# Attention's sums inverted as columns, expert weights split earlier, on one Trainium2 core

## The chip, the cores and the metric

One core of one Trainium2 chip runs the whole program. The metric is the device time of one execution in microseconds, taken as the median of the runs; in this kernel about 0.2% can be told from no change.

## The reference

```python
scores = q @ k.T / sqrt(64) + min(-(cum_i - cum_j), 0), causal    # cum: running sum of max(s, 0)
attn = exp(scores - max); attn = attn / (sum(attn) + 1e-9)
x = (attn @ v)                      # 4 batches, 8 heads, 576 positions, 64 per head
x = x.transpose(0, 2, 1, 3).reshape(2304, 512)
h = max(x @ w_in, 0); x = (h * h) @ w_out                         # 512 -> 2048 -> 512
h = max(x @ w1, x @ w2, x @ w3); out = h @ w_out2                 # 512 -> 768 -> 512
```

All inputs are float32, the weights come as 64-bit words (float64).

## The kernel before

**Attention** goes through 16 pairs of heads, each pair through nine units of 128 score rows (64 of each head for the ninth, unit 8). For a unit TensorE makes the scores (`u_s`, L508 to L518), VectorE adds the mask and takes the largest (`u_max`, L531), ScalarE takes the exponential in place and adds it up into a column of a small tile `sums` (`u_exp`, L545), TensorE transposes the exponentials into one of two PSUM banks (`u_t`, L590), and ScalarE copies them out as `et` (`u_et`, L617 to L622). Units 0 to 3 are window 0 of the pair, units 4 to 8 window 1. When a window is complete TensorE multiplies `et` with the values (`w_pv`, L642), and VectorE copies the product to `xT` (`w_out_`, L653).

The sums stand as columns, a row for a query. They are needed as rows. `u_t` transposes them (L597) into the last 64 columns of the bank that holds unit 5's, or unit 8's, exponentials; `w_cp` adds 1e-9 out of that bank (L556) and takes the reciprocal (L558), both on a tile of 4 or 5 rows and 128 columns; `w_keep` stores it in DRAM (L565, L567), `w_rows` fetches it back spread over 64 rows (L574), and `w_px` multiplies on GpSimd (L658).

The order is a table, `ORDER`: step n of the loop does, from left to right, each operation for unit n + d. `LOADS` says when the next pair's inputs are loaded, on the SP queue.

**The experts** work on `xT` in chunks of 512 or 384 tokens. Every float32 factor is split into a high part and a low rest in the type fp32r, and three products stand for one (`three`, L661). For tokens this is `split_x` (a cast on ScalarE, L665, a subtraction on VectorE, L666). The first stage goes through nine visits: chunks 0 to 3 with the first half of the 16 blocks of `w_in` and `w_out`, chunk 4 with all 16 (visit 4), chunks 3 to 0 with the second half. A block is an "h" step (12 products, L672) and, two steps later, an "x" step (12 products, L798). Between them: relu and square (L777, L778), split (L780, L781). At a visit's end the four sums are copied out (L808, L810). The second stage (L838, L879) has 24 weights. `first_split` and `first_products` do the first `PRE` = 2 "h" steps of chunk 0 at the end of attention.

**Weights.** A weight block becomes a split tile by a job (`w_job`) of nine stages: two loads, four steps on VectorE (L340 to L351) that turn the 64-bit words to a float, an addition (L355), a cast on ScalarE (L360), a subtraction (L363). The additions run on GpSimd during attention, on VectorE afterwards. An early job makes a second-stage weight in a spare tile and stores it to DRAM (L366); `w_bring` fetches it later on GpSimd's queue (L379). A planner, `Slots`, decides at each call of `pump`, when the program is written, which job goes a stage on and whether one begins: weights needed within `SOON` steps at once, others at most one per `pace`. Attention calls it in the steps of a pair that `PUMP_U` lists, and with `ADV_ATT` = 1 each call does one stage; the experts call it after every step.

## Time and profile before

| | |
|---|---|
| median of 3 runs | 896.93 us (896.42 to 897.15) |
| profiled execution | 896.98 us |
| its span | 895.2 us |
| TensorE, VectorE, ScalarE, GpSimd busy | 855.9, 514.3, 332.2, 66.9 us |
| granted TensorE clock, mean | 0.997 |

Times within the profile count from the span's start. Attention ends near 187 us, the first expert stage near 592, the rest is the second. A row of a timeline gives start, duration, engine, line, operation and, in brackets, how long the engine idled before and what released it. PE is TensorE, PEld its weight loads, DVE VectorE, ACT ScalarE, POOL GpSimd, SPq the SP queue.

### The profile page before, as it was taken

The numbers are of one execution on the slowest core, as the hardware profiler recorded it, in microseconds if no ns is written. First come the engines' busy times: TensorE is split into PE (matmuls) and PEld (weight loads), VectorE is DVE, ScalarE is ACT, GpSimd is POOL, SyncE is SP. The second block draws the span as 40 slices with busy tenths as digits, with TensorE's granted clock in tenths as the row PEclk, the third lists the DMA queues.
The fourth block names the chain that finished last, engine by engine and source line by source line (L and its number), as shares of the span: only waits on it lengthen the run. The fifth ranks groups of instructions, "written<-read, shape, count | busy, mean of one in ns | idle before, by whom it ended". The sixth has DMA issues, their size and how long they took to land.

```text
span 895.2 us, 14075 instructions
## 1 busy us (share of the span) xinstructions
PE 855.9 (96%) x5446; PEld 730.0 (82%) x5446; DVE 514.3 (57%) x1079; ACT 332.2 (37%) x729; POOL 66.9 (7%) x79
## 2 busy tenths in 40 slices
PE   5999888899899999998999999999999999999998
PEld 3555555577688899997998888899999999999997
DVE  6788797868886333788888777633223131312211
ACT  5788887843333223323333333311112120212111
POOL 2133333310000000000000000110000000000000
PEclk9999999999999999999999999999999999999999
DMA  4454545212321020432425355950000000000001
GB/s 144 152 151 126 177 125 166 86 57 94 125 88 47 1 83 1 142 95 94 130 69 196 116 190 184 318 151 1 13 24 1 36 1 36 1 25 12 12 24 36
DMA packets 45267, 79.00 MB, mean 88 GB/s; under 512 B 7568, under 2 KB 17360, under 8 KB 45200
## 3 DMA queue, kind: packets, MB, share of 16 engines
q1 hardware_dynamic: 42884, 69.70, 24.3%
q0 software_dynamic: 2304, 8.39, 3.1%
q8 instruction: 43, 0.70, 0.3%
q14 instruction: 24, 0.20, 0.1%
q10 hardware_dynamic: 12, 0.01, 0.0%
HBM read 60.84 MB, written 17.22 MB: 87 GB/s over the span
## 4 chain that ended last, share of the span: by engine, by line
PE 75%; DVE 14%; ACT 6%; issue 4%; DMA 1%; DVEq 0%; ACTq 0%
PE banks L838 17%; PE banks L798 16%; PE first L838 8%; PE banks L879 8%; PE first L672 8%; PE banks L672 8%; PE pairs L642 4%; PE pairs L590 3%; DVE e L531 2%; PE pair L508 2%; DVE st L351 2%; PE pairs L508 2%; DVE r L778 2%; ACT hh L780 2%; ACT et L619 2%
## 5 line engine op out<-in xcount | busy, mean ns | idle before, releaser
L798 PE MATMUL banks<-hh,sl 128*128 128x512 f32 (+1 forms) x840 | 187.1, 371 | 4.4 <-DVE pt L808 1.8
L798 PEld LDWEIGHTS banks<-hh,sl 128*128 128x128 f32 x840 | 153.9, 189 | 27.7 <-DVE pt L808 2.2
L838 PE MATMUL banks<-xs,sl 128*128 128x384 f32 x720 | 128.7, 334 | 0.0
L838 PEld LDWEIGHTS banks<-xs,sl 128*128 128x128 f32 x720 | 125.1, 188 | 0.0
L780 ACT CAST hh<-r 128x512 fp32r<-128x512 f32 (+1 forms) x80 | 46.2, 578 | 152.8 <-DVE r L778 152.8
L672 PE MATMUL banks<-xs,sl 128*128 128x512 f32 (+1 forms) x420 | 92.0, 367 | 0.0
L672 PE MATMUL first<-xs,sl 128*128 128x512 f32 (+1 forms) x396 | 87.2, 368 | 4.4 <-DVE xs L666 3.2
L545 ACT ACTIVATE e<-e,nm 128x128 f32<-128x128 f32 (+2 forms) x144 | 83.5, 582 | 11.9 <-DVE nm L531 11.5
L672 PEld LDWEIGHTS banks<-xs,sl 128*128 128x128 f32 x420 | 76.7, 188 | 9.9
L672 PEld LDWEIGHTS first<-xs,sl 128*128 128x128 f32 x396 | 72.3, 188 | 13.9 <-DVE xs L666 3.5
L781 DVE TENSOR_TENSOR hh<-r,hh 128x512 fp32r<-128x512 f32 (+1 forms) x80 | 51.1, 639 | 51.5 <-ACT hh L780 50.2
L854 DVE TENSOR_TENSOR r<-banks,r 128x384 f32<-128x384 f32 x54 | 30.1, 557 | 78.5 <-PE banks L838 78.0
L879 PE MATMUL banks<-sl,hh 128*128 128x512 f32 (+1 forms) x342 | 74.9, 378 | 0.0
L879 PEld LDWEIGHTS banks<-sl,hh 128*128 128x128 f32 x342 | 61.8, 188 | 11.8
L858 ACT CAST hh<-r 128x384 fp32r<-128x384 f32 x36 | 18.5, 513 | 138.4 <-DVE r L854 138.4
L590 PEld LDWEIGHTS pairs<-identF,e 64*128 64x128 f32 x800 | 33.4, 139 | 30.6 <-ACT et L619 23.2
L590 PE MATMUL pairs<-identF,e 64*128 64x64 f32 x800 | 41.4, 230 | 16.8 <-ACT et L619 16.5
L642 PEld LDWEIGHTS pairs<-et,xv 128*64 128x64 f32 (+1 forms) x448 | 27.8, 135 | 31.2 <-ACT e L545 8.3
L642 PE MATMUL pairs<-et,xv 128*64 128x320 f32 (+4 forms) x448 | 52.7, 367 | 0.0
L838 PE MATMUL first<-xs,sl 128*128 128x384 f32 x288 | 52.0, 335 | 0.0
L838 PEld LDWEIGHTS first<-xs,sl 128*128 128x128 f32 x288 | 50.3, 188 | 0.5
L854 DVE TENSOR_TENSOR r<-first,r 128x384 f32<-128x384 f32 x18 | 10.0, 558 | 67.3 <-PE first L838 67.3
(104 smaller groups left out, 1116.1 us busy)
## 6 DMA issues: line engine op xcount, KB each, us to landing
st<-in_w_out_dram SPq DMA_DIRECT2D x44, 256.0 KB
st<-in_w_dram SPq DMA_DIRECT2D x36, 256.0 KB
st<-in_w_in_dram SPq DMA_DIRECT2D x32, 256.0 KB
keep_w<-spare SPq DMA_DIRECT2D x10, 512.0 KB
xk<-in_kT_dram SPq DMA_DIRECT2D x16, 288.0 KB
xq<-in_qT_dram SPq DMA_DIRECT2D x16, 288.0 KB
out_dram<-ob SPq DMA_DIRECT2D x17, 256.0 KB
xv<-in_v_main_dram SPq DMA_DIRECT2D x16, 256.0 KB
```

Of the source, the lines that this page charges most:

```text
L508: nc.tensor.matmul(b[:, j, 0:w], lhsT=d["xq"][rows(j), w - P:w], rhs=d["xk"][rows(j), 0:w], start=True, stop=False)
L545: nc.scalar.activation(out=e_u[u][:, 0:w], in_=e_u[u][:, 0:w], func=ACTF.Exp, scale=-1.0, bias=st.pop(n), accum_out=sums[p, win][:, col:co ...
L590: nc.tensor.transpose(t[:, h, at * D:(at + 1) * D], e_u[v][rows(h), k * P:(k + 1) * P], identF[rows(h), rows(h)])
L642: nc.tensor.matmul(pv[rows(j), f:(W0, W1)[w]], lhsT=xv[0:kr, j, k, :], rhs=rhs, start=(k == 0), stop=(k == last))
L672: nc.tensor.matmul(hps[:, 0:n], lhsT=w[:, wp, kk * P:(kk + 1) * P], rhs=x[kk][xp][:, 0:n], start=(kk == 0 and c == 0), stop=(kk == KD - 1 ...
L780: nc.scalar.copy(out=hh[:, 0, 0:n], in_=r[:, 0:n])
L781: nc.vector.tensor_tensor(out=hh[:, 1, 0:n], in0=r[:, 0:n], in1=f32(hh[:, 0, 0:n]), op=ALU.subtract)
L798: nc.tensor.matmul(xacc[d][:, 0:n], lhsT=w[:, wp, d * P:(d + 1) * P], rhs=hh[:, xp, 0:n], start=(m == 0 and c == 0), stop=(end and c == 2))
L838: nc.tensor.matmul(pj[j][:, 0:n], lhsT=w[:, wp, kk * P:(kk + 1) * P], rhs=xs[kk][xp][:, 0:n], start=(kk == 0 and c == 0), stop=(kk == KD - ...
L854: nc.vector.tensor_tensor(out=r[:, 0:n], in0=p[:, 0:n], in1=r[:, 0:n], op=ALU.max)
L858: nc.scalar.copy(out=hh[:, 0, 0:n], in_=r[:, 0:n])
L879: nc.tensor.matmul(po[:, 0:hi - lo], lhsT=hs[ci, f][:, hp_, t * P:(t + 1) * P], rhs=w[:, wp, lo:hi], start=(c == 0), stop=(c == 3 * NF2 - 1))
```

## The change

Six things are done.

- The sums become reciprocals while they are columns (`w_rc`, on tiles of 128 x 4 or 5). One transpose per window behind the value products puts them into the second half of the product's bank, and `w_out_` copies them out behind the values.
- `w_keep` moves from unit offset -6 to -7, behind that copy.
- The planner is called in all nine steps of a pair (`PUMP_U`).
- Weights needed more than `FAR` = 24 steps ahead keep a pace of 3.
- Early jobs may run in every visit but 0, 1 and 4, where they could from the 81st step on (in visit 4).
- The first expert split is spread over attention's last 30 units, high part and low part in steps of their own; the first products begin one step earlier and go five per step, where they went three.

```diff
-PRE_X = 8
-PRE_AT = 0
-PRE_N = 3
-PUMP_U = (0, 2, 3, 4, 5, 7)
+PRE_X = (30, 21, 12, 5)
+PRE_AT = 1
+PRE_N = 5
+PUMP_U = range(9)
...
-EARLY_FROM = 80
+EARLY_NOT_IN = (0, 1, 4)
+FAR = 24
+PACE_FAR = 3
...
-ORDER = [("max", 1), ("cp", -3), ("out0", -6), ("out1", -7), ("exp", -1), ("et", -3), ("t", -2), ("s", 2), ("pv", -5), ("rows", -13),
-         ("pump", 0), ("keep", -6), ("px", -19)]
+ORDER = [("max", 1), ("out0", -6), ("out1", -7), ("rc", -3), ("exp", -1), ("et", -3), ("t", -2), ("s", 2), ("pv", -5), ("rows", -13),
+         ("pump", 0), ("keep", -7), ("px", -19)]
...
-                if n - self.pos > (SOON_KEPT if kept else SOON) and (kept or self.clock - self.last < self.pace):
+                pace = self.pace if n - self.pos <= FAR else max(self.pace, PACE_FAR)
+                if n - self.pos > (SOON_KEPT if kept else SOON) and (kept or self.clock - self.last < pace):
...
-        if not self.start() and self.idle_from is not None and self.pos >= self.idle_from and \
+        if not self.start() and self.pos in self.idle and \
...
-    def w_cp(p, w):
-        nu = U0 + w
-        sm = small.tile([NU - U0, P], F32, tag="rec", name="rec", bufs=2)
-        nc.vector.tensor_scalar(out=sm[0:nu, :].rearrange("u (h c) -> u h c", c=D), in0=tr_t.pop((p, w)), scalar1=1.0e-9,
-                                scalar2=None, op0=ALU.add)
-        nc.vector.reciprocal(out=sm[0:nu, :], in_=sm[0:nu, :])
-        rec_t[p, w] = sm
+    def w_rc(p, w):
+        sm = sums[p, w][:, 0:U0 + w]
+        nc.vector.tensor_scalar(out=sm, in0=sm, scalar1=1.0e-9, scalar2=None, op0=ALU.add)
+        nc.vector.reciprocal(out=sm, in_=sm)
...
-        if n in ends:
-            _, w = ends[n]
-            o = tr_t[p, w] = t[0:U0 + w, :, 7 * D:8 * D]
-            sm = sums.pop((p, w))
-            for h in range(2):
-                nc.tensor.transpose(o[:, h, :], sm[rows(h), 0:U0 + w], identF[rows(h), rows(h)])
...
+        sm = sums.pop((p, w))
+        nc.tensor.transpose(t[0:U0 + w, 1, 0:P], sm[:, 0:U0 + w], identF)
...
         nc.vector.tensor_copy(x, t[:, 0, 0:n])
+
+        sm = rec_t[p, w] = small.tile([NU - U0, P], F32, tag="rec", name="rec", bufs=2)
+        nc.vector.tensor_copy(sm[0:U0 + w, :], t[0:U0 + w, 1, 0:P])
         ring_t.give(t)
...
-            if n == N:
+            if n == N - PRE_AT:
                 phQ.close()
                 banks.extend(psum(ctx, "first", 2, [P, 512]))
-            if PRE and n >= N - PRE_X and (n - N + PRE_X) % 2 == 0 and (n - N + PRE_X) // 2 < KD:
-                first_split((n - N + PRE_X) // 2)
+            for kk in range(KD):
+                for later in range(2):
+                    if n == N - PRE_X[kk] + later:
+                        first_split(kk, later)
```

### Where instructions move

First place: ScalarE in the middle of attention, from the exponential of unit 6 to that of the next pair's unit 0. `et` are the copies of transposed exponentials, `e_152` to `e_154` the units 6 to 8. Before:

```order
L545 ACTIVATE e_152,sm_1221<-e_152,nm 128x512 [waits DVE_49]
L545 ACTIVATE e_153,sm_1221<-e_153,nm 128x512 [waits DVE_49]
L619 COPY et_1292<-pairs_91 128x2x6x64 [waits DVE_49,PE_49]
L545 ACTIVATE e_154,sm_1221<-e_154,nm 128x576
L545 ACTIVATE e_146,sm_1327<-e_146,nm 128x128 [waits Activation_49]
```

The change:

```order
L547 ACTIVATE e_152,sm_902<-e_152,nm 128x512 [waits DVE_49]
L364 CAST sl_69<-wa 128x512 [waits Pool_49]
L547 ACTIVATE e_153,sm_902<-e_153,nm 128x512 [waits DVE_49]
L609 COPY et_972<-pairs_91 128x2x6x64 [waits PE_49,Activation_49]
L547 ACTIVATE e_154,sm_902<-e_154,nm 128x576 [waits DVE_49]
L547 ACTIVATE e_146,sm_1012<-e_146,nm 128x128 [waits DVE_49,Activation_49]
```

The copy L619, L609 in the change, waits for TensorE and VectorE before, and for TensorE (and ScalarE itself) in the change.

Second place: the end of attention. First TensorE, from the transposes of the last unit (`e8`) to the first "h" step of the experts (`banks`); `first` are the banks of the first products. Before:

```order
L590 MATMUL pairs0_90<-identF_139,e8_154 128x64 x9
L597 MATMUL pairs0_90<-identF_139,sm1_2698 5x64 x2
L672 MATMUL first0_2787<-sl18_85,sl0_67 128x512 x3
...
L642 MATMUL pairs1_91<-et1_2757,xv_2552 64x320 x5
...
L672 MATMUL first1_2788<-sl18_85,sl1_68 128x512 x3
L672 MATMUL first1_2788<-sl17_84,sl1_68 128x512 x3
...
L672 MATMUL banks0_2865<-xs_2893,sl2_69 128x512 [waits DVE_49,Activation_49]
```

The change:

```order
L588 MATMUL pairs0_90<-identF_139,e8_154 128x64 x9
...
L673 MATMUL first1_2823<-sl18_85,sl1_68 128x512 x3
L673 MATMUL first1_2823<-sl17_84,sl1_68 128x512 x3
...
L632 MATMUL pairs1_91<-et1_2810,xv_2604 64x320 x5
...
L635 MATMUL pairs1_91<-identF_139,sm1_2756 5x128 [waits DVE_49]
L673 MATMUL banks0_2922<-xs_2950,sl2_69 128x512 [waits PE_49,Activation_49]
```

All 24 first products stand ahead of the last value products, where 12 stood behind them. On VectorE the same place reads, before:

```order
L556 TENSOR_SCALAR rec<-pairs_90 5x128 [waits DMAHW7_49,DMAHW6_49,PE_49]
L558 RECIPROCAL rec<-rec 5x128 [waits DVE_49]
L653 COPY xT<-pairs_91 128x320 [waits PE_49,Activation_49]
L666 TENSOR_TENSOR xs<-xT,xs 128x512 [waits DMAHW5_49,Activation_49]
L666 TENSOR_TENSOR xs<-xT,xs 128x512 [waits DMAHW5_49,DMAHW6_49,DMAHW2_49,Activation_49]
```

The change:

```order
L557 RECIPROCAL sm_2756<-sm_2756 128x5 [waits DVE_49]
L646 COPY xT<-pairs_91 128x320 [waits PE_49,Activation_49]
L649 COPY rec<-pairs_91 5x128 [waits DMAHW1_49,DMAHW0_49]
L663 TENSOR_TENSOR xs<-xT,xs 128x512 [waits DMAHW5_49,DMAHW4_49,Activation_49]
L663 TENSOR_TENSOR xs<-xT,xs 128x512 [waits DMAHW4_49,DMAHW7_49,DMAHW0_49,Activation_49]
```

The tile `rec` that goes to DRAM is complete before the last value copy in the one, behind it in the other. The second split of `xs` takes memory over from `rec` and waits, in both, for that store (the semaphores DMAHW).

Third place: VectorE at the end of visit 4 (the two splits in one row belong to its last block). Before:

```order
L348 TENSOR_SCALAR wa<-st 128x512
L351 SCALAR_TENSOR_TENSOR st<-st,wa 128x512
L355 TENSOR_TENSOR wa<-st 128x512
L340 TENSOR_SCALAR wa<-st 128x512
L344 SCALAR_TENSOR_TENSOR st<-st,wa 128x512
L666 TENSOR_TENSOR xs<-xT,xs 128x384 x2
L778 SCALAR_TENSOR_TENSOR r<-banks_2866,r 128x384
L781 TENSOR_TENSOR hh<-r,hh 128x384
L363 TENSOR_TENSOR sl_77<-wa,sl_77 128x512
L348 TENSOR_SCALAR wa<-st 128x512
```

The change:

```order
L663 TENSOR_TENSOR xs<-xT,xs 128x384
L367 TENSOR_TENSOR sl_74<-wa,sl_74 128x512
L782 SCALAR_TENSOR_TENSOR r<-first_2823,r 128x384
L785 TENSOR_TENSOR hh<-r,hh 128x384
L782 SCALAR_TENSOR_TENSOR r<-banks_2922,r 128x384
L785 TENSOR_TENSOR hh<-r,hh 128x384
L663 TENSOR_TENSOR xs<-xT,xs 128x384 x2
L782 SCALAR_TENSOR_TENSOR r<-banks_2923,r 128x384
L785 TENSOR_TENSOR hh<-r,hh 128x384
```

The weight work around the splits is gone there; it stands in visits 2 and 3, one job per two blocks, where there was none.

Over the program 56 jobs are made in both. On GpSimd, in attention, there are 15 of the additions L355 where there were 10, and 15 of the subtractions L363 where there were 9; 24 of the jobs are early ones where 16 were, and as many tiles are stored and fetched back.

## Rows read from the trace of the kernel before

**Rows 1.** The page: span of the profiled execution.

```profile
span 895.2 us, 14075 instructions
```

**Rows 2.** Windows of one pair each: length, then PE, PEld, DVE, ACT, POOL busy (14 windows).

```profile
161.43:173.38 11.95, 10.04 (x121) 5.83 (x118) 10.83 (x29) 8.91 (x22) 4.19 (x5) 1.00 0.38 107
...
sum 151.51, PE 135.87 PEld 80.92 DVE 123.89 ACT 123.20 POOL 49.97; mean PE 9.71 PEld 5.78 DVE 8.85 ACT 8.80 POOL 3.57
```

**Rows 3.** Groups by line, shapes apart, 22.59 to 186.82: busy us, mean ns, idle before.

```profile
L590 PE MATMUL pairs<-identF,e 64*128 64x64 f32 x746 | 38.5, 230 | 16.0 <-ACT et L619 15.7 <-ACT e L545 0.4
...
L558 DVE RECIPROCAL rec<-rec 4x128 f32<-4x128 f32 x15 | 14.1, 941 | 0.5
...
L619 ACT COPY et<-pairs 128x768 f32<-128x768 f32 x15 | 12.0, 799 | 12.9 <-DVE rec L556 11.3 <-PE pairs L642 1.6
...
L531 DVE DVE_READ_ACCUMULATOR2_ANT nm<- 128x1 f32 x130 | 9.9, 76 | 0.0
...
L351 DVE SCALAR_TENSOR_TENSOR st<-st,wa 128x512 f32<-128x512 uint32 x10 | 8.2, 816 | 0.0
...
L556 DVE TENSOR_SCALAR rec<-pairs 4x128 f32<-4x128 f32 x15 | 4.1, 274 | 0.2 <-issue 0.2
```

**Rows 4.** Timeline of ScalarE in the pair from 75.56.

```profile
81.08 0.80 ACT L619 COPY et<-pairs 128x768 f32<-128x768 f32 x1 [0.77 <-DVE rec L556]
```

**Rows 5.** The chain that ended last, in order of time: start, us, what.

```profile
249.59 2.72 PE first L672 x12
...
345.42 2.08 PE banks L672 x12
```

**Rows 6.** Timeline of TensorE at the end of visit 0.

```profile
217.56 2.88 PE L672 MATMUL banks<-xs,sl 128*128 128x512 f32 x12
221.08 3.38 PE L798 MATMUL banks<-hh,sl 128*128 128x512 f32 x12 [0.64 <-ACT sl L360]
...
241.81 2.34 PE L798 MATMUL banks<-hh,sl 128*128 128x512 f32 x9 [1.76 <-DVE pt L808]
243.98 2.88 PE L672 MATMUL banks<-xs,sl 128*128 128x512 f32 x12
```

**Rows 7.** Timeline of TensorE between visits 4 and 5; one window with its clock.

```profile
413.98 2.24 PE L798 MATMUL banks<-hh,sl 128*128 128x384 f32 x12
...
422.06 1.48 PE L672 MATMUL first<-xs,sl 128*128 128x384 f32 x5 [3.20 <-DVE xs L666]
...
436.64 0.68 PE L672 MATMUL banks<-xs,slb 128*128 128x384 f32 x3
...
424.00:426.00 2.00, 2.00 (x8) 0.50 0.00 0
```

**Rows 8.** Timeline of the engines at the end of attention.

```profile
182.62 0.94 DVE L558 RECIPROCAL rec<-rec 5x128 f32<-5x128 f32 x1
...
186.02 1.66 ACT L665 CAST xs<-xT 128x512 fp32r<-128x512 f32 x3 [2.18 <-DMA r<-rec]
...
186.82 2.35 PE L672 MATMUL first<-sl,sl 128*128 128x512 f32 x9
187.01 0.49 DVE L653 COPY xT<-pairs 128x320 f32<-128x320 f32 x1 [3.44 <-PE pairs L642]
187.41 3.72 DVE L666 TENSOR_TENSOR xs<-xT,xs 128x512 fp32r<-128x512 f32 x4
...
193.17 2.12 PE L798 MATMUL banks<-hh,sl 128*128 128x512 f32 x8 [0.23 <-DVE hh L781]
```

**Rows 9.** Groups by line over the whole run.

```profile
L351 DVE SCALAR_TENSOR_TENSOR st<-st,wa 128x512 f32<-128x512 uint32 x56 | 40.1, 716 | 1.6
...
L363 POOL TENSOR_TENSOR sl<-wa,sl 128x512 fp32r<-128x512 f32 x9 | 12.7, 1413 | 26.9 <-ACT sl L360 26.9
...
L355 POOL TENSOR_TENSOR wa<-st 128x512 f32<-128x512 f32 x10 | 10.4, 1039 | 19.4 <-DVE st L351 19.4
```

**Rows 10.** Window of visit 8: engines busy, clock, share of the transfer engines, GB/s.

```profile
560.00:570.00 10.00, 10.00 (x45) 8.27 (x45) 6.82 (x12) 2.90 (x6) 2.11 (x4) 1.00 1.05 353
```

More of the change, by code (lines that the diff above doesn't have):

```diff
@@ L107, in __init__ @@
         self.most = ADV_ATT
-        self.idle_from = None
+        self.idle = ()
     def add(self, tiles):
@@ L487 @@
     units = [(p, u) for p in range(NP) for u in range(NU)]
-    wins, ends = {}, {}
+    wins = {}
     for n, (p, u) in enumerate(units):
@@ L491 @@
             wins[n] = (p, int(u >= U0))
-        if u in (U0 + 1, NU - 1):
-            ends[n] = (p, int(u == NU - 1))
     st = {}
@@ L661, with high, low_of, split_x @@
     three = ((0, 0), (0, 1), (1, 0))
-    def split_x(t0, n, kk, high, low):
-        src = xT[:, kk, t0:t0 + n]
-        nc.scalar.copy(out=high[:, 0:n], in_=src)
-        nc.vector.tensor_tensor(out=low[:, 0:n], in0=src, in1=f32(high[:, 0:n]), op=ALU.subtract)
-        return high, low
+    def high(t0, n, kk, hi, lo):
+        nc.scalar.copy(out=hi[:, 0:n], in_=xT[:, kk, t0:t0 + n])
+    def low_of(t0, n, kk, hi, lo):
+        nc.vector.tensor_tensor(out=lo[:, 0:n], in0=xT[:, kk, t0:t0 + n], in1=f32(hi[:, 0:n]), op=ALU.subtract)
+    def split_x(t0, n, kk, hi, lo):
+        high(t0, n, kk, hi, lo)
+        low_of(t0, n, kk, hi, lo)
+        return hi, lo
     def h_products(hps, x, n, w):
@@ L677, with first_split @@
     first_x = {}
-    def first_split(kk):
-        if kk < HELD_BACK:
-            high, low = (slots_a[-1 - kk][:, i, :] for i in range(2))
-        else:
-            high, low = (hp.tile([P, S], F32R, tag=n, name=n)[:, 0:512] for n in ("xk", "xq"))
-        first_x[kk] = split_x(*chunks1[0], kk, high, low)
+    def first_split(kk, low):
+        if not low:
+            if kk < HELD_BACK:
+                first_x[kk] = tuple(slots_a[-1 - kk][:, i, :] for i in range(2))
+            else:
+                first_x[kk] = tuple(hp.tile([P, S], F32R, tag=n, name=n)[:, 0:512] for n in ("xk", "xq"))
+        (high if not low else low_of)(*chunks1[0], kk, *first_x[kk])
     def first_products():
@@ L695, in attention @@
         fns = dict(s=u_s, t=u_t, max=u_max, et=u_et, exp=u_exp)
-        efn = dict(cp=w_cp)
-        wfn = dict(pv=w_pv, out0=w_out_, out1=w_out_, keep=w_keep, rows=w_rows, px=w_px)
+        wfn = dict(rc=w_rc, pv=w_pv, pv0=w_pv, pv1=w_pv, out0=w_out_, out1=w_out_, keep=w_keep, rows=w_rows, px=w_px)
         span = max(abs(d) for _, d in ORDER)
@@ L715, in attention @@
                         slots.pump(1)
-                elif op in efn:
-                    if n + d in ends:
-                        efn[op](*ends[n + d])
                 elif op in wfn:
-                    if n + d in wins and op not in ("out1", "out0")[wins[n + d][1]]:
+                    if n + d in wins and op[-1] != "10"[wins[n + d][1]]:
                         wfn[op](*wins[n + d])
@@ L740, in experts @@
         adder[0] = nc.vector
-        slots.idle_from = EARLY_FROM
+        slots.idle = set(range(len(steps)))
+        for i, step in enumerate(main1):
+            if step[1] in EARLY_NOT_IN:
+                slots.idle.discard(i)
         slots.add(slots_a[-HELD_BACK:] + [sl_p.tile([P, 2, 512], F32R, name=f"slb{i}") for i in range(SLOTS_B)])
```

1 line of the change is left out of this document (removed).

## The prediction

> **What bounds the kernel now.** I read the page first, then the windows, the groups by line, and the timelines of the places where TensorE waits. The profiled execution took 896.98 us for a span of 895.2 us [rows 1], so 1.78 us lie outside the span; the median of the runs shown, 896.93, is the same within 0.05 us. Everything below is counted in the span and taken from 896.98. TensorE sets the end: a change is worth what it takes out of, or adds to, TensorE's own waits, and nothing else.
>
> Attention: between 33.28 and 184.79 us lie 14 pairs of heads of 151.51 / 14 = 10.82 us each; TensorE is busy for 9.71 of it, VectorE for 8.85, ScalarE for 8.80 [rows 2]. So 1.1 us per pair is lost, and the groups say to what: in the 15 pairs from 22.59 on, the transposes of exponentials (L590) wait 16.0 us, of that 15.7 for one copy on ScalarE, L619 [rows 3]. That copy itself waits: of its 12.9 us before the 768-wide form, 11.3 are for L556, the VectorE step that takes attention's sums out of the bank that L619 also reads [rows 3]. One such wait is seen at 81.08: 0.77 us [rows 4].
>
> Experts: twelve products take 2.72 us with 512 tokens and 2.08 with 384 where nothing waits [rows 5]. From 217.56 to 243.98 there are 8 such groups of 512, 21.76 us, in 26.42 us: 4.7 us lost, to weights that are not split yet (two waits like the one at 221.08) and to the last: copies out of the banks that stood behind weight work on VectorE [rows 6]. From 413.98 to 436.64 there are 7 groups of 384, 14.56 us, in 22.66: 8.1 us lost, mostly at 422.06, where the split of the next chunk stood behind weight work on VectorE; the clock then went to 0.50 for a while [rows 7]. I find no wait worth naming behind 437 up to the tail.
>
> **The change, term by term.**
>
> *The sums.* VectorE loses 32 adds of 274 ns and 32 reciprocals of 941 ns [rows 3]: 38.9 us. It gains 32 copies of 4 or 5 x 128 out of the bank, priced like the add, 0.27, and 64 operations on 4 or 5 columns, which the trace does not show; they lie between the 128x1 read of 76 ns and the 274 ns of the add [rows 3], and I take 0.1, near the first, since their width is nearer: 8.6 + 6.4 = 15 us. TensorE loses 64 transposes of 64 columns and gains 32 of 128: the same columns, so I take 0 (bounds: a gain of 2 us, or 0.1 us a pair more, 1.5 us). What counts is that L619 no longer waits for VectorE (first place of the order). ScalarE's copy then starts when ScalarE is free, and its 11.3 us are taken from TensorE's 15.7; 4.4 us stay. Bounds: all 15.7 gained, or 3, if ScalarE or the next wait is late instead. The next wait is named: the single's transposes need the bank that the copy of the values and now the copy of the sums, 0.27 us more, must have left; that is 0 to 0.27 x 15 = 4.1 us, and since other TensorE work stands between, I charge 1.0. **Attention: -10.3.**
>
> *Weights in every step.* The order has 15 weights whose halves are added on GpSimd in attention where it had 10. ScalarE gets about 6 more casts of 0.55 us [rows 8], 3.3 us over 15 pairs, 0.22 us a pair: 8.80 + 0.22 in a pair that is to last 10.82 - 10.3/15 = 10.1. VectorE gets 5 x 4 steps of at most 0.82 us [rows 3], 16.4 us, less than the 38.9 - 15 that it lost. Cover is there on both, though on ScalarE only a microsecond of it. Five more loads of 0.5 MB fall on the SP queue; nothing urgent stands behind them. GpSimd gets 5 adds of 1.04 us and 6 of 1.41 [rows 9]; who waits for them is the load of the next weight alone. In return the last first-half weight is begun before attention ends, so the waits of 217 to 244 lose their cause; I leave 0.5 us of the 4.7. **Visit 0: -4.2.**
>
> Where the weight work runs beside GpSimd, VectorE is slower: L351 takes 816 ns in attention against 716 over the run [rows 3, 9]. The Trainium skill ("Trainium Architecture — The Big Picture", section on what this means for kernel authors) says that VectorE and GpSimd share a port pair as an exclusive lock, which speaks against putting more adds there. By the row the price is 0.1 us an operation, 20 x 0.1 = 2 us, hidden; what the lock would make of it is a rival below.
>
> *Early weights.* All 24 weights of the second stage are now made ahead, where 16 were, and in visits 2, 3 and 5 to 8, none in visit 4. At visit 4's end VectorE had about one weight job (five or so steps) per expert block; the third place of the order shows none there now. The 8.1 us go; I leave 0.4. **-7.7.** In visits 2 and 3 there is a job per two blocks. A job is at most 6 x 0.72 = 4.3 us of VectorE (L351's 716 ns as the longest step, [rows 9]), a block's own work 1.2 us; 2.2 + 1.2 = 3.4 us per block against 4.16 us of TensorE: it fits, but tightly with the splits, so I charge **+1.0** (0 to 8.1). The 8 weights more that are fetched back replace 8 raw loads of the same size and 8 jobs, in a stretch where the transfer engines were at 1.05 of their time without TensorE waiting [rows 10]: 0.
>
> *The end of attention.* All 24 of the first products now stand ahead of the last value products on TensorE (second place of the order), where 12 stood behind them. That fills the wait in the last pair, but strips the cover behind it. The second split of the experts' tokens waits for the transfer that stores the last sums, since it takes over their memory: at 186.02 ScalarE had waited 2.18 us for it [rows 8]. So far that store followed a reciprocal that ended at 182.62 + 0.94 = 183.56; 2.46 us later the split began. Now it follows the last value products. Let E be their end (186.82 before). VectorE starts 0.19 later, copies values 0.49 and sums 0.27: E + 0.95; the split begins at E + 3.41. From the split to the second product of the first output block it was 193.17 - 186.02 = 7.15; of it fall away 0.84 (the low halves stood behind the value copy until 187.41) and 0.93 (one of four is done before): 5.38, so E + 8.79. TensorE has 13 products of 0.227 us until then, 2.95: 5.84 idle. Before, 6.35 us held 25 products, 5.67: 0.68 idle. **+5.1.** Bounds: +3, if the low halves run at 0.66 and the store lands a microsecond sooner; +6.3, if the clock halves after the idle stretch as it did at 424 [rows 7].
>
> Splits moved up (units 30, 21, 12, 5 before the end) are the same four casts and subtractions; beside attention's slack they cost 0.
>
> Sum: -10.3 - 4.2 - 7.7 + 1.0 + 5.1 = -16.1, so 896.98 - 16.1 = **880.9 us**.
>
> **Rivals.**
> - *ScalarE takes the wait's place* (0.17). For it: 9.0 us of work in a 10.1 us pair, in order, with casts of weights ahead of L619. Against: it idles 2.0 us a pair today. Attention then gains 3: 888.2.
> - *The lock* (0.06): the 11 added GpSimd adds stop VectorE whole, 5 x 1.04 + 6 x 1.41 = 13.7 us instead of 2, and VectorE's saving of 7.5 turns into 6.2 more, all exposed: 887.1. That is the skill's rule above taken literally; the 816 ns speak against it.
> - *The stall moves to visit 3* (0.10): early jobs there delay the split of visit 4 as it happened at 422, 8.1 instead of 1.0: 888.0.
> - *VectorE falls behind in attention* (0.05): the pair from 161.43 took 11.95 us with VectorE busy 10.83 [rows 2]. If the denser jobs make every pair like it, 1.13 x 15 = 17.0 us come instead of -10.3: 908.2, slower. It decides from 11.3 us a pair on: without attention's term the sum is 891.2, and 0.5 x 15 brings it to 898.8. Against it: VectorE loses more than it gets.
>
> My forecast has the rest, 0.62.
>
> **How the numbers follow.** A measurement of this kernel tells from no change about 0.2%, 1.8 us. Low end: all of 15.7 instead of 10.3 and +3 instead of +5.1 give 873.4, taken as 874; the high end takes in the first three rivals with 1.5 us on top: 890. Left out are the slower case and two rivals at once, under 0.2. Faster 0.93; slower 0.04, the last rival; same 0.03, its mild form or two of the others together.
>
> **What would show it.** Right: L619 no longer waits for VectorE and L590's idle falls from 16.0 towards 5; pairs near 10.1 us; no TensorE wait over half a microsecond in visit 0 and at visit 4's end; and a new TensorE gap of 4 to 6 us between the last value products and the first output block, with the split on ScalarE waiting for the store of sums. Wrong: pairs above 10.6 with ScalarE busy throughout, a gap at the end of visit 3, or no gap behind attention.

## The result, and the profile after

The changed kernel takes 888.56 us (median of 4 runs, 887.60 to 890.01) against 897.04 of the kernel before in the same measurement: a ratio of 0.990, 95% interval 0.988 to 0.992. The forecast was 880.9, the range 874 to 890: the range held, the gain is half of what was forecast, 8.5 us instead of 16.1. The profiled execution took 888.79 us.

First the page, then one window for each of 14 pairs (from the value products of window 1 in the first pair to those in the fifteenth; length, then PE, PEld, DVE, ACT, POOL busy, clock), which answer to [rows 1, 2]:

```profile
span 887.0 us, 14072 instructions
```

```profile
22.70:33.05 10.35, 10.05 (x119) 5.89 (x117) 7.48 (x29) 8.26 (x24) 0.00 (x0) 1.00 0.67 202
33.05:42.87 9.82, 9.82 (x118) 5.79 (x117) 9.00 (x35) 8.18 (x21) 3.90 (x5) 1.00 0.38 117
...
84.57:98.18 13.61, 11.05 (x118) 6.04 (x116) 10.62 (x36) 9.46 (x24) 4.12 (x4) 1.00 0.44 130
...
sum 150.71, PE 142.31 PEld 82.04 DVE 122.19 ACT 124.25 POOL 55.84; mean PE 10.17 PEld 5.86 DVE 8.73 ACT 8.87 POOL 3.99
```

The same 14 pairs took 150.79 us before (22.27 to 173.06). Attention, from which 10.3 us were to come, has not moved. But the wait that was to go has gone, as the groups by line of the changed kernel show (22.70 to 188.87; busy us, mean ns, idle before; lines shift a little: L588 was L590, L609 was L619, L364 was L360):

```profile
L588 PE MATMUL pairs<-identF,e 64*128 64x64 f32 x746 | 39.2, 230 | 4.5 <-DVE rec L649 1.8 <-ACT et L609 1.8 <-ACT e L547 0.4
...
L348 DVE SCALAR_TENSOR_TENSOR st<-st,wa 128x512 uint32<-128x512 uint32 x15 | 13.4, 893 | 0.0
...
L609 ACT COPY et<-pairs 128x768 f32<-128x768 f32 x15 | 11.7, 783 | 0.0
...
L556 DVE TENSOR_SCALAR sm<-sm 128x5 f32<-128x5 f32 x15 | 5.1, 341 | 0.7 <-ACT e L547 0.7
...
L635 PE MATMUL pairs<-identF,sm 128*4 128x128 f32 x15 | 4.1, 271 | 0.1
...
L556 DVE TENSOR_SCALAR sm<-sm 128x4 f32<-128x4 f32 x15 | 3.4, 226 | 0.0
L557 DVE RECIPROCAL sm<-sm 128x5 f32<-128x5 f32 x15 | 2.9, 191 | 0.5
L557 DVE RECIPROCAL sm<-sm 128x4 f32<-128x4 f32 x15 | 2.7, 178 | 0.5
```

L609 waits for nothing any more (12.9 us before), and L588 waits 4.5 us where L590 waited 16.0 [rows 3]. Instead the scores L510 wait 3.6 us for VectorE's L533, the mask and largest (0.6 before), and TensorE's recorded busy time per pair has grown: 10.17 us, where the 14 windows of [rows 2] have 9.71. A part of that is waiting too, as the last section shows.

Stage by stage, by the start of VectorE's first subtraction for `hh` (L781 before, L785 now) in a visit, and of the first in the second stage:

| stretch | before | after | difference | forecast |
|---|---|---|---|---|
| start to visit 0 | 192.4 | 196.3 | +3.9 | -10.3 + 5.1 = -5.2 |
| visits 0 to 3 | 161.0 | 157.2 | -3.8 | -4.2 + 1.0 = -3.2 |
| visits 4 and 5 | 109.9 | 101.1 | -8.8 | -7.7 |
| visits 6 to 8 | 136.7 | 137.6 | +0.9 | 0 |
| second stage | 295.1 | 294.7 | -0.4 | 0 |

The expert terms hold; 9.1 us are missing, all in the first row. Of TensorE's waits in visit 0 [rows 6] one is left, and of those at visit 4's end [rows 7] none:

```profile
241.99 2.33 PE L802 MATMUL banks<-hh,sl 128*128 128x512 f32 x9 [0.42 <-DVE pt L812]
```

The end of attention looks as forecast. Timeline of all engines, changed kernel:

```profile
188.62 0.28 PE L635 MATMUL pairs<-identF,sm 128*5 128x128 f32 x1
...
189.70 0.62 SPq L563 DMA_DIRECT2D r<-rec  x1
190.33 0.74 PE L673 MATMUL banks<-xs,sl 128*128 128x512 f32 x2 [1.21 <-DVE xs L663]
...
192.45 1.66 ACT L660 CAST xs<-xT 128x512 fp32r<-128x512 f32 x3 [8.26 <-issue]
193.10 1.90 DVE L663 TENSOR_TENSOR xs<-xT,xs 128x512 fp32r<-128x512 f32 x3 [2.83 <-ACT xs L660]
193.12 4.11 PE L673 MATMUL banks<-xs,sl 128*128 128x512 f32 x9 [2.06 <-ACT xs L660]
...
197.07 1.18 PE L802 MATMUL banks<-hh,sl 128*128 128x512 f32 x4
```

Let E be the end of the last transpose (L635), 188.90, for which VectorE's copies wait; the prediction counted from the end of the value products, 188.69 here. The split was forecast at E + 3.41 = 192.31 and began at 192.45, after the store of the sums (L563). The second product of the first output block was forecast at E + 8.79; the block's first product came at E + 8.17, its second at E + 8.41. Of those 8.41 us 13 products fill 2.95: 5.5 us of TensorE are lost, part of them as a halved clock (granted 0.50 in the window from 194 to 196; length, then PE, PEld, DVE, ACT, POOL busy, clock):

```profile
194.00:196.00 2.00, 2.00 (x5) 1.61 (x6) 1.60 (x3) 0.97 (x3) 1.34 (x2) 0.50 0.56 158
```

### The profile page after: what moved, and what is told of

Same layout as the page of the kernel before. It is cut to its first block, busy times and chain, and to the rows that moved or that the text cites. A ratio compares the mean times of both kernels' runs of the same rounds, so it can differ in the third digit from the quotient of the medians.

```text
span 887.0 us, 14072 instructions
## 1 busy us (share of the span) xinstructions
PE 862.3 (97%) x5414; PEld 732.0 (83%) x5414; DVE 492.9 (56%) x1100; ACT 331.3 (37%) x729; POOL 80.5 (9%) x98
## 4 chain that ended last, share of the span: by engine, by line
PE 85%; DVE 8%; ACT 2%; issue 2%; DMA 1%; POOL 0%; SPq 0%; DVEq 0%; ACTq 0%; POOLq 0%
PE banks L802 20%; PE banks L842 17%; PE first L673 10%; PE banks L673 10%; PE first L842 8%; PE banks L883 8%; PE pairs L632 4%; PE pairs L588 2%; PE pair L510 2%; DVE e L533 1%; PE pairs L510 1%; DVE st L348 1%; PE pair L517 1%; DVE st L355 1%; ACT e L547 1%
## 5 line engine op out<-in xcount | busy, mean ns | idle before, releaser
L802 PE MATMUL banks<-hh,sl 128*128 128x512 f32 (+1 forms) x840 | 184.4, 368 | 0.4 <-DVE pt L812 0.4
L673 PE MATMUL banks<-xs,sl 128*128 128x512 f32 (+1 forms) x420 | 94.4, 372 | 3.3 <-ACT xs L660 2.1
L785 DVE TENSOR_TENSOR hh<-r,hh 128x512 fp32r<-128x512 f32 (+1 forms) x80 | 51.4, 642 | 51.6 <-ACT hh L784 50.2
L781 ACT ACTIVATE r<-first 128x512 f32<-128x512 f32 (+1 forms) x40 | 22.1, 554 | 75.7 <-PE first L673 75.7
L588 PEld LDWEIGHTS pairs<-identF,e 64*128 64x128 f32 x800 | 33.7, 139 | 19.6 <-ACT et L609 6.9
```

The costliest lines, as they stand in the source:

```text
L588: nc.tensor.transpose(t[:, h, at * D:(at + 1) * D], e_u[v][rows(h), k * P:(k + 1) * P], identF[rows(h), rows(h)])
L673: nc.tensor.matmul(hps[:, 0:n], lhsT=w[:, wp, kk * P:(kk + 1) * P], rhs=x[kk][xp][:, 0:n], start=(kk == 0 and c == 0), stop=(kk == KD - 1 ...
L781: nc.scalar.activation(out=r[:, 0:n], in_=hps[:, 0:n], func=ACTF.Relu)
L785: nc.vector.tensor_tensor(out=hh[:, 1, 0:n], in0=r[:, 0:n], in1=f32(hh[:, 0, 0:n]), op=ALU.subtract)
L802: nc.tensor.matmul(xacc[d][:, 0:n], lhsT=w[:, wp, d * P:(d + 1) * P], rhs=hh[:, xp, 0:n], start=(m == 0 and c == 0), stop=(end and c == 2))
```

## The experiments

Theories after this look. **Given back:** the sums' gain is real and was eaten, by TensorE's new transposes, by weights whose loads have not landed, or by small VectorE steps beside GpSimd. **Weight work:** the denser jobs ate it, by their number or by the places in the pair where they now stand. **The forecast's rivals:** ScalarE or VectorE as a whole is the new bound. All diffs are against the changed kernel unless said; "pairs" is the time of the 14 pairs above, from each run's profiled execution.

| run | median us | ratio to before (95%) | pairs us |
|---|---|---|---|
| the change | 888.56 | 0.9903 (0.9883 to 0.9924) | 150.71 |
| e5_sums | 886.69 | 0.9871 (0.9858 to 0.9885) | 139.51 |
| e6_pump6 | 878.44 | 0.9782 (0.9763 to 0.9800) | 139.82 |
| e4_delay | 884.65 | 0.9849 (0.9835 to 0.9862) | 147.52 |
| e11_place | 886.93 | 0.9889 (0.9863 to 0.9914) | 149.73 |
| e12_few | 881.98 | 0.9830 (0.9812 to 0.9847) | 146.01 |
| e13_hold | 876.82 | 0.9751 (0.9731 to 0.9771) | 140.01 |
| e2_half | 885.18 | 0.9866 (0.9844 to 0.9887) | 150.66 |
| e3_noeps | 886.48 | 0.9869 (0.9855 to 0.9884) | 148.62 |
| e9_rec | 883.98 | 0.9844 (0.9826 to 0.9863) | 149.18 |
| e7_early | 900.18 | 1.0020 (1.0005 to 1.0034) | 148.47 |
| e10_best | 870.74 | 0.9702 (0.9686 to 0.9719) | 136.99 |
| e14_best | 867.82 | 0.9657 (0.9636 to 0.9678) | 134.89 |

The runs come from several measurements, in which the kernel before took 897.0 to 898.6 us; so a difference between the medians of two runs is uncertain by up to 1.5 us, and the ratios compare better. The attention program of e7 and e9 is the change's own, and their pairs take 148.5 and 149.2: some 2 us of a single profile hang on when loads land. It is the pair from 84.57 that differs: 13.61 us in the change, 11.16 in e7 and e9.

### The sums alone

```diff
-PRE_X = (30, 21, 12, 5)
-PRE_AT = 1
-PRE_N = 5
-PUMP_U = range(9)
+PRE_X = (8, 6, 4, 2)
+PRE_AT = 0
+PRE_N = 3
+PUMP_U = (0, 2, 3, 4, 5, 7)
...
-EARLY_NOT_IN = (0, 1, 4)
-FAR = 24
+EARLY_NOT_IN = ()
+FAR = 1 << 20
...
-        slots.idle = set(range(len(steps)))
+        slots.idle = set(range(80, len(steps)))
...
-                    if n == N - PRE_X[kk] + later:
+                    if n == N - PRE_X[kk]:
```

> The kernel before, with the sums' part of the change alone (columns inverted, turned behind the value products, copied behind the values, stored a step later); planner, splits, first products as before. By the prediction's own term attention gains 10.3 and the end of attention costs 1 to 3: 888 to 890. If the gain is given back on TensorE (4.8 us) and by VectorE's small steps (about 2), but no load is late as the planner is the old one: about 897 - 11.5 + 4.8 + 2 + 1.5 = 893.8. If ScalarE takes the wait's place: 897 - 3 + 1.5 = 895.5.

Windows by pair of e5_sums:

```profile
22.43:32.26 9.83, 9.83 (x118) 5.80 (x116) 6.29 (x26) 8.11 (x24) 0.00 (x0) 1.00 0.70 223
...
91.56:101.88 10.32, 10.02 (x119) 5.79 (x117) 6.42 (x28) 8.97 (x26) 4.08 (x4) 1.00 0.56 171
101.88:111.70 9.82, 9.82 (x118) 5.79 (x117) 7.08 (x30) 8.14 (x24) 2.22 (x3) 1.00 0.64 201
...
sum 139.51, PE 138.41 PEld 81.34 DVE 108.68 ACT 119.38 POOL 43.28; mean PE 9.89 PEld 5.81 DVE 7.76 ACT 8.53 POOL 3.09
```

The sums give 11.3 us in 14 pairs, a little more than the prediction's term; 11 of the 14 pairs are 9.82 or 9.83 us, with TensorE busy throughout. "ScalarE takes the wait's place" as a bound by its whole work is dead: it has 8.53 us of work in 9.97. This one part of the change is worth at least as much as all of it, so the rest of the change loses in attention what it wins behind it.

### The planner's calls

```diff
-PUMP_U = range(9)
+PUMP_U = (0, 2, 3, 4, 5, 7)
```

> The changed kernel with the planner called in six of a pair's nine steps as before (0, 2, 3, 4, 5, 7); sums, early weights, splits and first products as changed. With the sums' part alone 14 pairs took 139.5 us, with the whole change 150.7. If the denser weight work ate the gain, pairs come back to about 9.83 and attention gives 10.9; visit 0 gets its waits back, 3.7: 888.6 - 10.9 + 3.7 = 881.4. If it was not the weight work but the splits or the 24 first products moved ahead, the pairs stay near 10.76 and with visit 0's waits the time is 892.

878.44, and the pairs are back at 139.82 us. So the weight work costs the 11 us, and not the splits or the first products. Visit 0 gets two waits back, 0.64 and 0.55 us; the first in TensorE's timeline of e6_pump6:

```profile
214.19 3.38 PE L802 MATMUL banks<-hh,sl 128*128 128x512 f32 x12 [0.64 <-ACT sl L364]
```

The third wait, for copies at the visit's end [rows 6], stays away. Visits 0 to 3 take 159.5 us here, 2.3 more than in the change: that is all that the extra weights in attention bought.

### Late loads, number, or place

Four runs take the weight work apart. Longer delays:

```diff
-DELAY_ATT = (2, 6, 2, 2, 2, 2, 4, 0, 1, 1)
+DELAY_ATT = (3, 9, 2, 2, 2, 2, 4, 0, 1, 1)
```

> The changed kernel, with the planner's delays between a weight's load and its first step back at the length in steps that they had (2 and 6 calls, six calls in nine steps, before; here 3 and 9 calls, nine in nine). In the trace of the change VectorE stands 4.6 us in attention before L344 for weights that have not landed, and TensorE's waits for L533 lie behind it. If those waits cost attention its gain, VectorE's wait goes and 2 to 4 us come back: 885 to 887. With 12 weights finished in attention instead of 15, visit 0 may wait for a split again, 0.6 us or two of them. If VectorE's density is what costs, it falls with the number of jobs, to the same effect but without waits for loads being the reason: then e3 gains as well. If TensorE's transposes explain all of it, no change: 888.6.

VectorE's wait for loads is gone. The row of the waits in the changed kernel (us in total, times, longest), which has no counterpart in e4_delay:

```profile
DVE wa L344 <- issue: 4.6, 2, 2.9
```

The profile names no releaser here ("issue"). That it is a load follows from the longer delay, with which the wait goes, and from e11_place below, where 1.8 us of waits in the same line are put down to the load of `st`. 888.56 becomes 884.65 and the pairs 147.52: 3.2 of the 11 us come back. How much of that is the loads is not shown exactly, since the longer delays also leave 13 additions in attention instead of 15 and put the work in other steps. Some eight us are left.

The same calls in the old steps:

```diff
-PUMP_U = range(9)
+PUMP_U = (0, 2, 2, 3, 4, 4, 5, 7, 7)
...
-                    if PUMP_FROM <= n < N + PUMP_END and n % NU in PUMP_U and (slots.free or slots.open):
-                        slots.pump(1)
+                    for _ in range(PUMP_U.count(n % NU)):
+                        if PUMP_FROM <= n < N + PUMP_END and (slots.free or slots.open):
+                            slots.pump(1)
```

> The changed kernel with the planner called nine times a pair as in the change, but only in the old six steps (0, 2, 2, 3, 4, 4, 5, 7, 7): the same number of weights are begun, with the same delays in calls, and no weight step is issued in steps 1, 6 and 8. If the number of weights made in attention is what costs (density), pairs stay near 10.76 and the time near 888.6. If it is the steps in which the work now stands (weight steps ahead of the largest L533 and of the exponentials), pairs come down to about 10 and the time to 879 to 881. If it is the loads that have not landed, nothing changes in the delays, and the time stays within 2 us.

886.93, nearly unchanged, which looks like a verdict for number. It is none: here the loads are waited for as well, and three of the calls fall into steps 2, 4 and 7 twice. Pairs of 9.83 us stand beside pairs of 11 and 12, which a count of weights does not explain.

Fewer weights:

```diff
-DELAY_ATT = (2, 6, 2, 2, 2, 2, 4, 0, 1, 1)
+DELAY_ATT = (3, 9, 2, 2, 2, 2, 4, 0, 1, 1)
...
-PACE_ATT = 5
+PACE_ATT = 16
```

> The run with longer delays (e4, 884.65 us, 14 weights begun in attention), with a pace that begins 11 in attention; the planner is still called in all nine steps. If it is the number of weights made in attention that costs, about 2 us for each (8 us between 10 in e5 and 14 in e4), three fewer give 5 to 6 us back in attention and up to 1.3 us are lost to waits in visit 0: 879 to 881. If it is work in steps 1, 6 and 8 that costs, each pair with such a step keeps its 0.5 to 1 us, and the time stays at 882 to 885.

881.98, but the pairs take 146.01 where 2 us a weight would have given 141.5. Three weights fewer are worth 1.5 us there. Number falls, and the pairs themselves say why. Below, for some pairs of e12_few, what the planner issues in which of the pair's nine steps (e, c, p, r: VectorE's four steps; W: the addition; H: the cast on ScalarE; L: the subtraction on GpSimd; loads left out):

```
start   pair    4   5   6   7   8   0   1   2   3
 32.14  10.99   e   c   c   p   p   r   r   W   W
 74.81  10.84   W   -   -   H   L   H   L   -   -
 85.65   9.82   -   e   -   c   -   p   -   r   e
106.36  10.32   -   -   -   H   L   -   -   e   -
126.50   9.83   -   H   L   e   -   c   -   p   -
```

A cast in step 5 costs nothing; one in step 7 costs 0.49, two (7 and 0) 1.01. (The expectation of e13_hold below gives 1.0 for a cast in step 1. That was misread: in those pairs a cast of the experts' split stands too, in step 6, and each of the two costs 0.5.) Two timelines of e5_sums show how, ScalarE and TensorE's L588. First the pair with a cast in step 7, then the next one, without (a few rows left out):

```profile
94.62 0.80 ACT L607 COPY et<-pairs 128x768 f32<-128x768 f32 x1 [1.34 <-PE pairs L588]
95.32 0.72 ACT L547 ACTIVATE e<-e,nm 128x512 f32<-128x512 f32 x1
...
96.04 0.61 ACT L364 CAST sl<-wa 128x512 fp32r<-128x512 f32 x1
96.55 0.72 ACT L547 ACTIVATE e<-e,nm 128x512 f32<-128x512 f32 x1
...
97.26 0.78 ACT L609 COPY et<-pairs 128x768 f32<-128x768 f32 x1
...
98.10 0.71 PE L588 MATMUL pairs<-identF,e 64*128 64x64 f32 x16 [0.30 <-ACT et L609]
```

```profile
104.94 0.80 ACT L607 COPY et<-pairs 128x768 f32<-128x768 f32 x1 [1.68 <-PE pairs L588]
105.63 0.72 ACT L547 ACTIVATE e<-e,nm 128x512 f32<-128x512 f32 x1
...
106.35 0.71 ACT L547 ACTIVATE e<-e,nm 128x512 f32<-128x512 f32 x1
...
107.05 0.78 ACT L609 COPY et<-pairs 128x768 f32<-128x768 f32 x1
...
108.05 0.71 PE L588 MATMUL pairs<-identF,e 64*128 64x64 f32 x16
```

ScalarE's idle time in a pair is one piece, the 1.68 us ahead of L607. From there on its operations stand end to end, and TensorE waits for the end of that row: the bank that L609 empties. From L607 to L609 it is 2.64 us with the cast and 2.11 without, and TensorE's transposes stand still for it. The pair is 10.32 us long instead of 9.82.

So the test of place: work in the harmful steps is held back to the next harmless one.

```diff
-DELAY_ATT = (2, 6, 2, 2, 2, 2, 4, 0, 1, 1)
+DELAY_ATT = (3, 9, 2, 2, 2, 2, 4, 0, 1, 1)
...
+        if self.at is not None and (job.at == 7 and self.at not in (2, 3, 4, 5) or job.at in (2, 3, 4, 5) and self.at == 1):
+            return False
         need = job.takes.get(job.at)
...
-                        slots.pump(1)
+                        slots.at = n % NU
+                        slots.pump(1)
+                        slots.at = None
```

> The kernel of e4 (nine calls, longer delays), with two rules more for the planner in attention: a weight's cast on ScalarE is issued in steps 2 to 5 of a pair only, and none of its four VectorE steps in step 1. It begins 12 weights in attention, one more than e12. Laid side by side, the pairs of the runs so far take 9.83 us unless a cast falls in step 7, 8 or 0 (0.48 more), in step 1 (1.0 more) or a VectorE step in step 1 (0.5 more). If place is what costs, 14 pairs take 139 to 141 us (e12: 146.0, e4: 147.5) and the time falls from e12's 882.0 to 876 or 877. If the number of weights costs, the 14 pairs stay at 146 or above and the time at 882 or above.

876.82, and the pairs take 140.01 us, with more weights in attention (12 additions and 11 casts) than e12_few (10 and 10), which took 146.01. Windows of e13_hold:

```profile
31.63:41.45 9.82, 9.82 (x118) 5.79 (x116) 9.38 (x33) 8.11 (x24) 3.15 (x3) 1.00 0.39 122
...
90.59:100.41 9.82, 9.82 (x118) 5.80 (x116) 7.16 (x29) 8.63 (x25) 3.82 (x5) 1.00 0.47 154
...
sum 140.01, PE 138.45 PEld 81.34 DVE 114.95 ACT 120.62 POOL 47.07; mean PE 9.89 PEld 5.81 DVE 8.21 ACT 8.62 POOL 3.36
```

The first ten pairs are all 9.82 or 9.83, the one from 31.63 with VectorE busy for 9.38 of it; of the last four, three have a cast of the experts' split in step 6. Place it is. The rule has two parts, casts and VectorE's steps. This run does not take them apart; for the casts e14_best does, below. That a VectorE step in step 1 costs 0.5 us is read from pairs. The one from 74.23 in the changed kernel has such a step, an r, and no cast in a harmful place; it takes 10.34 us. VectorE and TensorE there:

```profile
82.21 0.69 DVE L355 SCALAR_TENSOR_TENSOR st<-st,wa 128x512 f32<-128x512 uint32 x1
...
82.81 0.42 DVE L533 CUSTOM_DVE_ANT_0 e<-pairs,bound 128x256 f32<-128x256 f32 x1
...
83.30 1.13 PE L510 MATMUL pairs<-xk,xq 64*128 64x512 f32 x4 [0.30 <-DVE nm L533]
```

The mask and largest of a unit (L533) stand behind the r, and TensorE's scores L510 wait for them: they begin 9.07 us into the pair, and 8.60 in the undisturbed pair from 101.88 of e5_sums. In the pair from 32.14 of e12_few the r in step 1 takes 1.33 us, beside an addition on GpSimd, and the pair is 1.16 us too long; the pair from 31.63 of e13_hold has the same steps (6c, 7p, 8p, 0r) without it and loses nothing.

Counted by these places, the 14 pairs of the change have nine VectorE steps in step 1, seven casts of weights in steps 6, 7, 8, 0 and 1, and three casts of the split in step 6. At 0.5 us each that is 9.5 us, an estimate from the pairs above; the pair from 84.57 has 2.5 more by a late load. Together they are 12.0 of the 13.1 us that the 14 pairs take beyond 9.83 each.

### The transposes and the small steps

```diff
-        nc.tensor.transpose(t[0:U0 + w, 1, 0:P], sm[:, 0:U0 + w], identF)
+        for h in range(2):
+            nc.tensor.transpose(t[0:U0 + w, h, 7 * D:8 * D], sm[rows(h), 0:U0 + w], identF[rows(h), rows(h)])
...
-        nc.vector.tensor_copy(sm[0:U0 + w, :], t[0:U0 + w, 1, 0:P])
+        nc.vector.tensor_copy(sm[0:U0 + w, :].rearrange("u (h c) -> u h c", c=D), t[0:U0 + w, :, 7 * D:8 * D])
```

> The changed kernel, with the sums turned by two transposes of 64 rows, each into its own bank, where one of 128 rows stood; all else is the same. In the trace of the change the 128-row transpose holds TensorE for 205 ns from start to start, a 64-row one of before for 56 ns a pair: 0.149 us in each of 32 windows, 4.8 us. If that is where attention's gain went (given back on TensorE), pairs come down by 0.3 us to about 10.45, and the time from 888.6 to about 884. If VectorE sets the pair (its weight steps are denser now), the 4.8 us turn into waits for L533 and the time stays within 1 us of 888.6. If ScalarE sets it, the same: 888.

885.18, 3.4 us less, in runs that lie further apart than the others (883.96 to 888.58; the profiled one, 888.29, has two pairs of 12.2 and 14.4 us). Its undisturbed pair is 9.60 us, against 9.83: the transposes are 0.23 us a pair. They are not what ate the gain, since e5_sums has them too.

The second edit leaves out the 1e-9 that is added to the sums:

```diff
     def w_rc(p, w):
         sm = sums[p, w][:, 0:U0 + w]
-        nc.vector.tensor_scalar(out=sm, in0=sm, scalar1=1.0e-9, scalar2=None, op0=ALU.add)
         nc.vector.reciprocal(out=sm, in_=sm)
```

> The changed kernel without the addition of 1e-9 to the sums (L556), which this kernel leaves out; the reciprocal stays. In the trace of the change the 30 additions take 8.5 us of VectorE (226 ns on 4 columns, 341 on 5, up to 895 beside GpSimd work). If small steps on VectorE that run slowly beside GpSimd make it late for TensorE, about 2 to 3 us come back: 886. If only TensorE's own transposes and weights that have not landed cost the gain, VectorE has slack for these steps and the time stays: 888.6 within 1. If VectorE's whole work sets the pair, all 8.5 come back: 880.

886.48, 2 us less by the medians, the time of the first case. The profile does not bear that case out: the 14 pairs take 148.62 us, and those of e7_early and e9_rec, which keep the addition, 148.47 and 149.18. So a cost of the small steps is not shown. VectorE's whole work does not set the pair: the 8.5 us did not come back.

### The end of attention and the early weights

```diff
-        sm = rec_t[p, w] = small.tile([NU - U0, P], F32, tag="rec", name="rec", bufs=2)
+        sm = rec_t[p, w] = perm.tile([NU - U0, P], F32, tag="rec", name="rec", bufs=2)
```

> The changed kernel with the tile of sums' rows (rec) in memory of its own, so that the experts' second split of tokens no longer waits for the store of the last sums; it still waits for the last value products, over whose factors it lies. In the trace of the change the value products end at 188.87 and the split begins at 192.45. If the store holds the split, it begins some 3 us sooner, 0.2 after the products, and 2.5 to 3.2 us of TensorE's 5.3 us gap go: 885.4 to 886.1. If the gap costs less than it shows (the clock's halving, VectorE's copies), under 1 us: 888.

The timeline of e9_rec at that place:

```profile
187.08 0.28 PE L635 MATMUL pairs<-identF,sm 128*5 128x128 f32 x1
...
187.44 1.66 ACT L660 CAST xs<-xT 128x512 fp32r<-128x512 f32 x3 [4.81 <-PE pairs L635]
...
188.79 2.77 PE L673 MATMUL banks<-xs,sl 128*128 128x512 f32 x11 [1.21 <-DVE xs L663]
...
191.84 0.50 PE L802 MATMUL banks<-hh,sl 128*128 128x512 f32 x1 [0.28 <-ACT hh L784]
```

The split begins 0.1 us after E (187.36), and the first output block comes at E + 4.5 instead of E + 8.2: 3.7 us. The time is 883.98, 4.6 less; the pairs were 1.5 shorter in its profile, by loads. The store held the split, as the prediction had it.

```diff
-        slots.idle = set(range(len(steps)))
+        slots.idle = set(range(80, len(steps)))
...
-EARLY_NOT_IN = (0, 1, 4)
-FAR = 24
+EARLY_NOT_IN = ()
+FAR = 1 << 20
```

> The changed kernel with the old rule for early weights (from the 81st step of the experts on, so that 16 are made ahead, in visit 4 too) and without the limit FAR. If the stall at the end of visit 4 came from weight work in that visit, it is back: 3.2 us for the split, the rest for copies and the halved clock, 7.7 in all, and the time is 896.3. If the splits moved because attention ends with more weights held, the stall stays away or is smaller: 889 to 892.

900.18, no faster than the kernel before (ratio 1.0020). The stall is back to the digit, in TensorE's timeline of e7_early:

```profile
424.01 1.85 PE L673 MATMUL first<-xs,sl 128*128 128x384 f32 x5 [3.20 <-DVE xs L663]
```

Visits 4 and 5 take 110.0 us, 8.9 more than in the change. Visits 0 to 3 take 161.9, 4.7 more: that was not expected. The trace shows the same stall in visit 0: at 228.63 TensorE has waited 1.87 us for a split of `xs` that stands behind six weight steps on VectorE, and from 230 to 232 the granted clock is 0.50. With 15 weights begun in attention but without the new rules the gain of visit 0 is gone (e5_sums, with the old rules and 10 weights, takes 161.6); with the rules and the old planner calls (e6_pump6) they take 159.5. So visit 0's gain hangs more on the rules than on the weights made in attention. Which of the two, the limit on far weights or the early jobs, was not run apart; since neither kernel lets early jobs run in visit 0, the limit on far weights is the likelier.

### Put together

e10_best joins e6_pump6, e2_half and e9_rec, and puts half of the first products behind the last value products again (`PRE_AT = 0`, `PRE_N = 3`).

> The changed kernel with four edits together: the planner called in six steps (e6, 878.44 us), two 64-row transposes (e2), rec in memory of its own (e9), and half of the first products behind the last value products again. Pairs lie at TensorE's floor of 9.83 us in e6, so the transposes should come off in full there, 0.24 x 15 = 3.6 (the shortest pair was 9.60 in e2); the store 2.5 to 4; twelve products of 0.227 us, 2.7, fill what is left of the gap. If all add up: 878.4 - 3.6 - 3.2 - 2.3 = 869.3. If VectorE or ScalarE sets the pairs once TensorE has less, pairs stay at 9.83 and the time near 873.

870.74. Ten of its 14 pairs are 9.60 or 9.61 us. The longer ones have a cast in step 7, or the casts of the experts' split, which stand in step 6. e14_best moves those:

```diff
-PRE_X = (30, 21, 12, 5)
+PRE_X = (33, 24, 15, 5)
```

and has the rule of e13_hold.

> The kernel of e10 (870.74 us) with the two rules of e13, and the casts of the experts' first split moved from step 6 of a pair to step 3 (33, 24, 15 and 5 units before the end). In e10 the pairs beyond 9.60 us are one with a weight's cast in step 7 (0.52 more) and four with the casts of the split (0.52, 1.03, 0.52, 0.48). If place is what costs, four of the five lose their excess, 2.0 to 2.5 us in all: 868.5. If the number of operations costs, they only move: 870.7.

867.82, 3.4% below the kernel before (ratio 0.9657) and 20.7 us below the change. Three of the five long pairs are 9.60 us now, one of the 14 stays at 10.09. e10_best has no VectorE step of a weight in step 1, and e14_best makes as many weights in attention (10 additions, 9 casts): the 2.1 us between their pairs go to the place of the casts. TensorE's timeline at the end of attention has no gap left:

```profile
166.81 2.42 PE L635 MATMUL pairs<-et,xv 128*64 128x320 f32 x20
169.17 0.22 PE L639 MATMUL pairs<-identF,sm 64*5 64x64 f32 x2
169.32 2.33 PE L677 MATMUL first<-sl,sl 128*128 128x512 f32 x9
...
172.17 2.88 PE L677 MATMUL banks<-xs,sl 128*128 128x512 f32 x12
```

## Why the prediction was half right

The range held, but not for its mechanism: its high end took in the first three rivals, and none of the three came as described. Of the signs named for being right, L590's idle time, the waits in visit 0 and at visit 4's end, and the gap behind attention came; pairs near 10.1 us did not.

**The sums, -10.3: right, by two errors that cancel.** e5_sums measures -11.3 over 14 pairs. Of TensorE's 15.7 us of waits "4.4 us stay" was too much: L609 waits for nothing in e5_sums, and L588 only 1.3 us. That the transposes have "the same columns, so I take 0" was wrong: one of 128 rows keeps TensorE 205 ns from start to start, the two of 64 rows 56 ns together, 0.149 x 32 = 4.8 us by the trace, 0.23 x 15 = 3.5 us by the shortest pairs. It was outside the bounds given (1.5). The small steps on VectorE, taken at 0.1 us, are 0.18 to 0.34 us in the change, 14.1 us in all where 6.4 were taken. The wait for the copy of the sums, charged at 1.0, is 1.8 us in the change (L588 for L649) and is not seen in e5_sums.

**"Weights in every step", 0 in attention: the step that failed.** It cost 11 us (150.7 against 139.8 in e6_pump6). The text had summed ScalarE's 9.0 us in a 10.1 us pair and found cover "on both". The cover is there as a sum and not where the work was put: ScalarE's slack is one piece of 1.7 us ahead of L607, and a cast behind it moves L609, and with it TensorE, by its whole length. On VectorE a weight's step in step 1 moves L533, for which TensorE's scores wait. e13_hold shows that place is what costs by moving the work, and gets back to 140.0. Up to about 3 us of the 11 were late loads (e4_delay): six calls were nine steps before and are six steps now, so a delay counted in calls had become shorter. The text counted the calls and did not carry the count over to the delays.

**The rival "ScalarE takes the wait's place"** gave 888.2, and 888.56 was measured. It had one of the two engines right; its mechanism, the sum of ScalarE's work, is refuted by e13_hold (8.62 us of ScalarE in pairs of 10.0). I put it at 0.17 because "it idles 2.0 us a pair", a number that says nothing of where.

The Trainium skill ("Perfetto Trace Analysis", section "Identifying the Most-Contended Engine") has occupancy as a fair measure of how near ScalarE and VectorE are to their limit. In the changed kernel's pairs ScalarE shows 8.87 us of 10.76 and still holds TensorE up wherever a cast stands behind L607: in this case the share misleads, and the row of operations without a gap decides.

**Visit 0, -4.2, and visits 2 and 3, +1.0:** -3.8 together, as forecast, but the cause was only half named (e7_early). **Early weights, -7.7:** right; e7_early brings the stall back. **The end of attention, +5.1:** right in size (5.5 us of TensorE lost, 0.7 before) and cause (e9_rec). That it could be avoided with 1 KB of memory per partition was not seen.

**The lock:** far from the rival's price, and near the forecast's 2 us for another reason. The 0.1 us an operation was a mean over steps with and without GpSimd beside them. In the kernel before, L351 takes 0.62 to 0.68 us with GpSimd idle and up to 1.26 beside it. What the four steps of all weights take beyond their time alone is 4.7 us in attention before and 6.3 in the change: 1.6 more, where the forecast had 2 and the rival 13.7. The additions to the sums, 3.8 us of the same kind, the forecast did not count.

**The stall in visit 3** did not happen: between 242 and 456 us the trace shows no wait of TensorE. **VectorE falling behind** did not happen as a limit either: the pair from 31.63 of e13_hold has VectorE busy for 9.38 of 9.82 us and is as short as any. (In that rival 891.2 + 7.5 is 898.7, not 898.8; nothing hangs on it.)

## What to carry to other kernels

Before you call added work covered on an in-order engine, find the gap that it would stand in: a total of idle time is no cover if it lies in one piece and the consumer waits at the end of the row behind it. When a schedule is called more often, convert every delay that is counted in calls. And when a change of many parts moves the time little, run its parts alone: here one part was worth as much as the whole.
